# One chunk's x split moved ahead, LN centring one step later and mixers 24 steps apart, in a three-layer kernel on one core

## The chip, the cores and the metric

One core of one Trainium2 chip runs the whole program: landmark attention, an MLP block with a low-rank token mixer, and an MLP block with a Fourier mixer. The metric is the device time of one execution in microseconds (us). Engines are named TensorE (PE in the rows, PEld its weight loads), VectorE (DVE), ScalarE (ACT), GpSimd (POOL) and SyncE (SP), which issues nearly all DMAs. TensorE's granted clock stands in the rows as a share of 2.4 GHz.

## What is computed

Batch 8, sequence 576, width 512, MLP width 2048. The attention's output is x of the first block, and that block's output is x of the second:

```
x    = attn(q, k, v)                       # landmark attention, (8, 576, 512)
u1   = x + (x^T U V)^T                     # U 576x32, V 32x576
x1   = u1 + relu(u1 @ w11) @ w12
u2   = x1 + real(fft over sequence and width of x1)
un   = (u2 - mean(u2)) / sqrt(var(u2) + 1e-6)
out  = u2 + relu(un @ w21) @ w22
```

Everything is fp32. A product of two fp32 operands is made of three TensorE passes over operands that are split into a high and a low part (`hi = cast(src)`, `lo = src - hi`): low times high, high times low, high times high.

## The kernel before

**MLP passes.** The 4608 tokens are nine chunks of 512. Each block's MLP is run as two passes over half the hidden width, since the weights of one half fit in SBUF: passes 0 and 1 make x1, passes 2 and 3 make the output. `Mlp.stream(p)` is a generator that emits one pass in *MLP steps* (it yields after each): a chunk is sixteen of them, and every step is twelve TensorE matmuls of 512 columns. Steps 0 to 7 are the up projection (`up`, L213 to L215: weights times high x, low weights times high x, weights times low x; then relu on ScalarE, L217, and the low part of g on VectorE, L218). Steps 8 to 15 are the down projection, two steps for each of four output blocks d (L258 to L260), each block ended by an eviction from PSUM: L267 on VectorE in passes 1 and 3, L265 on ScalarE in pass 2. The matmul results go through three PSUM banks, so a bank must be empty again two steps after its last matmul.

**x of the next chunk.** `load` brings xf, four tiles of 128x512, in step 3 of passes 1 to 3. `split_x` makes high and low parts of one tile at each call: the cast L51 on ScalarE, the subtraction L52 on VectorE for tiles 0 and 2, on GpSimd for tiles 1 and 3. The generator `more` is called at each of the eight stops of the down projection; it is created at d == 2, so the four tiles are split in steps 12 to 15. The four x tiles are single: they come free when the up projection has read them.

**Mixers.** Beside passes 1 and 2 run eight `Mixer`s, one for each batch: load U (one batch of x1), fold over width and sequence (the Fourier transform's symmetry), small DFT matmuls, unfold, add, store u2, and the LN. `Mixer.steps()` gives each piece a number; `Slots` runs the pieces of number r in MLP step `first + r`, right after that step of the MLP. The numbers that matter here: 0 load U; 4 the folds over width (L692: even part on VectorE, odd part on GpSimd); 5 to 8 the fold over sequence (L702) and splits, among them of one row (L713, `rh`, `rl`); 8 to 13 the DFT over width; 14 to 18 that over the sequence; 17 to 19 unfold; 20 store. LN follows for two halves n of the sequence: `sum_u` at 20 + n (two additions on VectorE, L782 and L783), `centre` at 21 + n (a mean by a matmul with a constant, L787, and the subtraction L797 on VectorE), `sum_sq` at 22 + n (square L802 on ScalarE, sums on VectorE), `put` of the centred half at 23 + n, `deviation` at 24 + n (again a mean, then L810 to L813 on ScalarE and L814 on GpSimd), `newton` at 25 + n (L818, L819 on VectorE) and `put_scale` at 26 + n. U has one buffer, so the next batch's load waits for this batch's second `centre`.

**Staging.** A third generator, `later`, converts the weights of the next passes from float64 to split fp32 (`stage`, `convert`): per weight tile four VectorE instructions (L96, L97, L100, L103) with L101 on ScalarE and L104 on GpSimd, then L106 on VectorE, then a split. It is advanced twice in steps divisible by 4 and once in others, and a weight tile takes ten advances, that is eight MLP steps.

**What sets the order.** Each engine runs its own instructions in the order in which they are emitted: MLP step, mixer pieces, constants' set-up, staging. An instruction that has to wait holds up all behind it on its engine. The mixers are put down by

```
for b in range(B):
    slots.add(34 + 22 * b, Mixer(fp, psb, f, b).steps())
```

counted from the first step of pass 1; a pass has 144 steps, so mixer 5 begins with pass 2. In what follows "mixer b" is that of batch b, and "mixer step r" the MLP step in which its pieces of number r are emitted.

Of the kernel before, what the change touches and what calls it, by code (L numbers as in the profile page):

```python
# [39 lines left out]
def body(ctx: ExitStack, tc: tile.TileContext, qT, kT, vn, mU, mV, w11, w12, w21, w22,  # L40
# [88 lines left out]
    def rows(d):  # L129
        return slice(d * P, (d + 1) * P)  # L130
# [33 lines left out]
    class Mlp:  # L164
# [57 lines left out]
        def stream(self, p, tail=None):  # L222
            x_src, res_src, dst, _ = self.passes[p]
            for c in range(NCH):
# [3 lines left out]
                after = (p, c + 1) if not last else (p + 1, 0) if p + 1 < len(self.passes) else None  # L228
# [20 lines left out]
                for d in range(4):  # L249
                    if d == 1 and after and p == 0:  # L250
                        self.xf = self.load(after[1], self.passes[after[0]][0])
                    if d == 2 and after:
                        more = self.split_x(self.xf)
                    ps = self.bank()
                    for k in range(HM):
                        gh, gl = g[k][:, 0, :], g[k][:, 1, :]
                        wh, wl = w2[k][:, 0, rows(d)], w2[k][:, 1, rows(d)]
                        nc.tensor.matmul(ps, wh, gh, start=k == 0, stop=False)  # L258
                        nc.tensor.matmul(ps, wl, gh, start=False, stop=False)  # L259
                        nc.tensor.matmul(ps, wh, gl, start=False, stop=k == HM - 1)  # L260
                        if k == HM // 2 - 1:
                            next(more, 0)
                            yield 1
                    if res_src is None:
                        nc.scalar.copy(res[d], ps)  # L265
                    else:
                        nc.vector.tensor_tensor(res[d], ps, res[d], op=ALU.add)  # L267
                    if tail:
                        nc.vector.tensor_tensor(res[d], res[d], sc, op=ALU.mult)
                        nc.vector.tensor_tensor(res[d], res[d], skip[d], op=ALU.add)  # L270
                    dst.put(c, d, res[d])
                    next(more, 0)
                    yield 1
# [396 lines left out]
    class Mixer:  # L670
# [156 lines left out]
        def steps(self):  # L827
            yield from ((0, self.load), (4, lambda: self.fold_d("e")), (4, lambda: self.fold_d("o")),
                        (5, lambda: self.fold_t("e")), (6, lambda: self.fold_split("e")), (6, self.fold_row),
                        (7, lambda: self.fold_t("o")), (8, lambda: self.fold_split("o")))  # L830
            yield from ((8 + 3 * (nm == "o") + i, lambda nm=nm, i=i: self.over_d(nm, i)) for nm in "eo"
                        for i in range(3))
            yield from ((14, self.top_row), (15, lambda: self.odd(0)), (16, lambda: self.even(0)),
                        (17, lambda: self.unfold(0)), (17, lambda: self.unfold(2)), (17, lambda: self.odd(1)),
                        (18, lambda: self.even(1)), (19, lambda: self.unfold(1)), (19, lambda: self.unfold(3)),
                        (20, self.store))
            for n in range(2):
                yield from ((20 + n, lambda n=n: self.sum_u(n)), (21 + n, lambda n=n: self.centre(n)),
                            (22 + n, lambda n=n: self.sum_sq(n)), (24 + n, lambda n=n: self.deviation(n)),
                            (23 + n, lambda n=n: self.put(n)),  # L840
                            (25 + n, lambda n=n: self.newton(n)), (26 + n, lambda n=n: self.put_scale(n)))

        LAST = 28

    def pool(name, **k):
        return tc.tile_pool(name=name, bufs=1, reuse_waits="tile", **k)
# [35 lines left out]
    N = NCH * STEPS  # L882
    with pool("mm") as mp, pool("pm", space=PSUM) as pm:
# [33 lines left out]
        with pool("aa") as ap_, pool("ac") as ac, pool("cv0") as cv0, pool("pt", space=PSUM) as psb:  # L917
            t = {}
            batches = [Batch(ap_, psb, t, b) for b in range(B)]
            slots = Slots()  # L920
# [30 lines left out]
        with tc.manual_schedule(), pool("cv") as cv:  # L951
            with pool("fp") as fp, pool("fc") as fc, pool("pf", space=PSUM) as psb:
                f = {}
                slots = Slots()
                for b in range(B):
                    slots.add(34 + 22 * b, Mixer(fp, psb, f, b).steps())
                later, gen = staging(cv, 2), mlp.stream(1)
                setup = fourier_setup(f, fc, fp)
                for s in range(N + 80):
                    if s == N:  # L960
                        some(later, 999)
                        some(gen, 9)
                        later, gen = staging(cv, 3), mlp.stream(2)
                    next(gen)
                    slots.run(s)
                    next(setup, 0)
                    some(later, 2 if s % 4 == 0 else 1)
            assert not slots.at
            for s in range(N - 80):
                next(gen)  # L970
                some(later, 2 if s % 4 == 0 else 1)
            some(later, 999)
            some(gen, 9)
            with pool("tl") as mlp.tail_pool:
                for _ in mlp.stream(3, (Scales(rs), U2)):
                    pass
# [75 lines left out]
```

## Time and profile before

| | us |
|---|---|
| median of 3 runs | 2014.88 |
| the three runs | 2014.88, 2016.48, 2009.8 |
| the profiled execution | 2012.54 |
| its span, first to last instruction | 2010.8 |

In the span TensorE is busy for 1900.4 us (95%), its weight loads for 1540.5, VectorE for 948.5, ScalarE for 552.9 and GpSimd for 356.1; the mean granted clock is 0.976. Consecutive matmuls overlap, and a busy engine need not be at its peak rate, so how long a step takes is read from the starts of its matmuls. Below, a stretch always runs from the first matmul of one MLP step to that of another; pass 1 begins at 682.14 us of the span, pass 2 at 1164.50 and pass 3 at 1613.29. A timeline row gives the start, the duration, engine, line and operation, what is written and read, and in brackets how long the engine was idle before it and what ended that.

### The profile page before, as it was taken

How to read it: one execution, taken by the hardware profiler on the slowest of the kernel's cores; microseconds unless marked ns; L12 is line 12 of the kernel's file. 1: busy time of each engine (PE TensorE's matmuls, PEld its weight loads, DVE VectorE, ACT ScalarE, POOL GpSimd, SP SyncE). 2: the span in 40 equal slices, each digit the busy share in tenths (PEclk: the TensorE clock that was granted, in tenths of full speed). 3: DMA queues.
4: the chain of work that ended last, by engine and by line, in shares of the span. 5: the costliest groups of instructions: out<-in, count | busy, mean ns of one | idle time of the engine just before them, and what ended most of it. 6: DMA issues, size and time to landing. Idle time of an engine off the chain costs nothing.

```text
span 2010.8 us, 27221 instructions
## 1 busy us (share of the span) xinstructions
PE 1900.4 (95%) x10808; PEld 1540.5 (77%) x10808; DVE 948.5 (47%) x1628; ACT 552.9 (27%) x1145; POOL 356.1 (18%) x344
## 2 busy tenths in 40 slices
PE   3568999999999999999999999999999999999998
PEld 2356777777778888778878777888888888888887
DVE  6795465556433334555466355464422233333333
ACT  2333332333322222233233233333322211111110
POOL 2441011111111112122222121221211110001000
PEclk8689999999999999989999999999999999999999
DMA  6224335343333743344354463343232453432332
GB/s 245 88 102 128 120 108 171 112 145 107 103 125 127 235 134 134 102 158 143 123 169 144 155 228 106 115 158 130 91 105 90 141 178 114 131 96 90 94 100 74
DMA packets 145873, 262.33 MB, mean 130 GB/s; under 512 B 22768, under 2 KB 77904, under 8 KB 145744
## 3 DMA queue, kind: packets, MB, share of 16 engines
q1 hardware_dynamic: 141248, 251.14, 37.6%
q10 hardware_dynamic: 4496, 9.44, 1.2%
q8 instruction: 85, 1.39, 0.3%
q14 instruction: 44, 0.36, 0.1%
HBM read 166.93 MB, written 93.59 MB: 130 GB/s over the span
## 4 chain that ended last, share of the span: by engine, by line
PE 75%; DVE 8%; DMA 7%; issue 3%; ACT 2%; POOL 2%; ACTq 0%; SPq 0%; POOLq 0%; DVEq 0%
PE ps L215 12%; PE ps L213 12%; PE ps L214 12%; PE ps L258 10%; PE ps L260 10%; PE ps L259 10%; DMA u<-u1T 5%; PE ps_f L76 1%; PE ps_f L77 1%; PE ps_f L78 1%; PE ps_n L572 1%; PE ps_n L613 1%; POOL x L52 1%; DMA xf<-u 1%; PE ps_c L443 1%
## 5 line engine op out<-in xcount | busy, mean ns | idle before, releaser
L213 PE MATMUL ps<-x,w 128*128 128x512 f32 x1152 | 466.8, 405 | 3.9 <-ACT x L51 3.9
L215 PE MATMUL ps<-x,w 128*128 128x512 f32 x1152 | 455.7, 396 | 7.6 <-POOL x L52 7.0
L258 PE MATMUL ps<-g,w 128*128 128x512 f32 x1152 | 460.1, 399 | 0.9 <-DVE g L218 0.9
L214 PE MATMUL ps<-x,w 128*128 128x512 f32 x1152 | 453.5, 394 | 0.0
L260 PE MATMUL ps<-g,w 128*128 128x512 f32 x1152 | 449.7, 390 | 0.0
L259 PE MATMUL ps<-g,w 128*128 128x512 f32 x1152 | 448.8, 390 | 0.0
L218 DVE SCALAR_TENSOR_TENSOR g<-ps,g 128x512 fp32r<-128x512 f32 x288 | 199.0, 691 | 463.0 <-ACT g L217 462.1
L217 ACT ACTIVATE g<-ps 128x512 fp32r<-128x512 f32 x288 | 171.9, 597 | 681.1 <-PE ps L215 680.6
L215 PEld LDWEIGHTS ps<-x,w 128*128 128x128 f32 x1152 | 218.9, 190 | 61.1 <-POOL x L52 12.8
L213 PEld LDWEIGHTS ps<-x,w 128*128 128x128 f32 x1152 | 219.3, 190 | 53.1 <-ACT x L51 4.9
L258 PEld LDWEIGHTS ps<-g,w 128*128 128x128 f32 x1152 | 216.3, 188 | 49.4 <-issue 4.4
L214 PEld LDWEIGHTS ps<-x,w 128*128 128x128 f32 x1152 | 219.5, 191 | 43.6
L260 PEld LDWEIGHTS ps<-g,w 128*128 128x128 f32 x1152 | 216.2, 188 | 46.7
L259 PEld LDWEIGHTS ps<-g,w 128*128 128x128 f32 x1152 | 216.5, 188 | 42.9
L104 POOL TENSOR_TENSOR cvp<-cvp,cva 128x512 f32<-128x512 f32 x64 | 83.3, 1301 | 692.0 <-DVE cvp L103 692.0
L267 DVE TENSOR_TENSOR xf<-ps,xf 128x512 f32<-128x512 f32 x108 | 74.4, 689 | 259.7 <-PE ps L260 256.8
L52 POOL TENSOR_TENSOR x<-xf,x 128x512 fp32r<-128x512 f32 x70 | 94.3, 1351 | 375.0 <-ACT x L51 373.4
L52 DVE TENSOR_TENSOR x<-xf,x 128x512 fp32r<-128x512 f32 x74 | 57.5, 779 | 114.8 <-ACT x L51 114.4
L51 ACT CAST x<-xf 128x512 fp32r<-128x512 f32 x144 | 85.4, 618 | 59.0 <-DMA xf<-u 58.8
L52 POOL TENSOR_TENSOR stg<-cva,stg 128x512 fp32r<-128x512 f32 x48 | 66.6, 1387 | 125.7 <-ACT stg L51 124.4
L572 PE MATMUL ps_n<-ry 128*128 128x192 f32 (+1 forms) x192 | 43.3, 352 | 35.1 <-DVE ry L576 35.1
L101 ACT ACTIVATE wraw<-wraw 128x512 f32<-128x512 f32 x50 | 34.1, 681 | 140.8 <-DVE cva L97 140.7
(276 smaller groups left out, 1750.6 us busy)
## 6 DMA issues: line engine op xcount, KB each, us to landing
wraw<-w SPq DMA_DIRECT2D x50, 512.0 KB
d<-stg SPq DMA_DIRECT2D x48, 512.0 KB
w<-d SPq DMA_DIRECT2D x48, 512.0 KB
y<-xf SPq DMA_DIRECT2D x72, 256.0 KB
xf<-y SPq DMA_DIRECT2D x72, 256.0 KB
U<-x SPq DMA_DIRECT2D x8, 1152.0 KB
u<-U SPq DMA_DIRECT2D x8, 1152.0 KB
un<-Z SPq DMA_DIRECT2D x16, 576.0 KB
```

The costliest lines, as they stand in the source:

```text
L51: nc.scalar.copy(hi, src)
L52: (eng or nc.vector).tensor_tensor(lo, src, f32(hi), op=ALU.subtract)
L104: nc.gpsimd.tensor_tensor(pf, pf, af, op=ALU.add)
L213: nc.tensor.matmul(ps, wh, xh, start=k == 0, stop=False)
L214: nc.tensor.matmul(ps, wl, xh, start=False, stop=False)
L215: nc.tensor.matmul(ps, wh, xl, start=False, stop=k == 3)
L217: nc.scalar.activation(g[:, 0, :], ps, AF.Relu)
L218: nc.vector.scalar_tensor_tensor(out=g[:, 1, :], in0=ps, scalar=0.0, in1=f32(g[:, 0, :]), op0=ALU.max, op1=ALU.subtract)
L258: nc.tensor.matmul(ps, wh, gh, start=k == 0, stop=False)
L259: nc.tensor.matmul(ps, wl, gh, start=False, stop=False)
L260: nc.tensor.matmul(ps, wh, gl, start=False, stop=k == HM - 1)
L267: nc.vector.tensor_tensor(res[d], ps, res[d], op=ALU.add)
```

## The change

In passes 1 to 3 the generator that splits x of the next chunk is created at the first block of the down projection instead of the third, so its four tiles are split in steps 8 to 11 (pass 0 keeps 12 to 15). In the mixer `centre` and all that follows it come one step later, while `sum_u` stays. The mixers begin at step 33 and then every 24 steps, instead of at 34 and every 22; the loops' bounds follow.

```diff
--- before.py
+++ after.py
@@ -249,7 +249,7 @@
                 for d in range(4):
                     if d == 1 and after and p == 0:
                         self.xf = self.load(after[1], self.passes[after[0]][0])
-                    if d == 2 and after:
+                    if d == (0 if p else 2) and after:
                         more = self.split_x(self.xf)
                     ps = self.bank()
                     for k in range(HM):
@@ -835,10 +835,10 @@
                         (18, lambda: self.even(1)), (19, lambda: self.unfold(1)), (19, lambda: self.unfold(3)),
                         (20, self.store))
             for n in range(2):
-                yield from ((20 + n, lambda n=n: self.sum_u(n)), (21 + n, lambda n=n: self.centre(n)),
-                            (22 + n, lambda n=n: self.sum_sq(n)), (24 + n, lambda n=n: self.deviation(n)),
-                            (23 + n, lambda n=n: self.put(n)),
-                            (25 + n, lambda n=n: self.newton(n)), (26 + n, lambda n=n: self.put_scale(n)))
+                yield from ((20 + n, lambda n=n: self.sum_u(n)), (22 + n, lambda n=n: self.centre(n)),
+                            (23 + n, lambda n=n: self.sum_sq(n)), (25 + n, lambda n=n: self.deviation(n)),
+                            (24 + n, lambda n=n: self.put(n)), (26 + n, lambda n=n: self.newton(n)),
+                            (27 + n, lambda n=n: self.put_scale(n)))
 
         LAST = 28
 
@@ -953,10 +953,10 @@
                 f = {}
                 slots = Slots()
                 for b in range(B):
-                    slots.add(34 + 22 * b, Mixer(fp, psb, f, b).steps())
+                    slots.add(33 + 24 * b, Mixer(fp, psb, f, b).steps())
                 later, gen = staging(cv, 2), mlp.stream(1)
                 setup = fourier_setup(f, fc, fp)
-                for s in range(N + 80):
+                for s in range(N + 88):
                     if s == N:
                         some(later, 999)
                         some(gen, 9)
@@ -966,7 +966,7 @@
                     next(setup, 0)
                     some(later, 2 if s % 4 == 0 else 1)
             assert not slots.at
-            for s in range(N - 80):
+            for s in range(N - 88):
                 next(gen)
                 some(later, 2 if s % 4 == 0 else 1)
             some(later, 999)
```

**ScalarE, the end of pass 1's chunk 3** (L51 `x<-xf` is the cast of x, `stg` and L101 are staging, L802 and L810 to L813 the LN, `he` and `rh` the fold's splits, L217 the first relu of chunk 4). Before:

```order
L51 CAST x<-xf 128x512
L101 ACTIVATE wraw<-wraw 128x512
L51 CAST x<-xf 128x512
L699 COPY cc<-big 128x2x2
L51 CAST x<-xf 128x512
L51 CAST he<-cc 128x578
L714 COPY top<-U 1x2
L51 CAST rh<-top 1x289
L51 CAST stg<-cva 128x512
L51 CAST x<-xf 128x512
L699 COPY cc<-big 128x2x2
L217 ACTIVATE g<-ps 128x512
```

Now, from the last relu of chunk 3 on:

```order
L217 ACTIVATE g<-ps 128x512
L51 CAST x<-xf 128x512
L802 ACTIVATE big<-Z 128x1152
L51 CAST x<-xf 128x512
L802 ACTIVATE big<-Z 128x1152
L51 CAST x<-xf 128x512
L810 ACTIVATE r<-ps_l,eps 128x288
L811 ACTIVATE v<-ps_l,eps 128x288
L812 ACTIVATE r<-r 128x288
L813 ACTIVATE w<-r 128x288
L51 CAST x<-xf 128x512
```

The four casts moved from among staging and fold to among the LN of the mixer before, and the staging and the fold come behind them.

**VectorE, the LN of one mixer in the up projection** (`cc<-U` and `cc<-cc` are `sum_u`, L797 `centre`, L218 the MLP's). Before (mixer 5):

```order
L782 TENSOR_TENSOR cc<-U 128x2x288
L783 TENSOR_TENSOR cc<-cc 128x288
L96 TENSOR_SCALAR cva<-wraw 128x512
L97 SCALAR_TENSOR_TENSOR cva<-wraw,cva 128x512
L100 TENSOR_SCALAR cvp<-cva 128x512
L103 SCALAR_TENSOR_TENSOR cvp<-wraw,cvp 128x512
L218 SCALAR_TENSOR_TENSOR g<-ps,g 128x512
L797 TENSOR_TENSOR Z<-U,ps_l 128x1152
L782 TENSOR_TENSOR cc<-U 128x2x288
L783 TENSOR_TENSOR cc<-cc 128x288
```

Now (mixer 2):

```order
L782 TENSOR_TENSOR cc<-U 128x2x288
L783 TENSOR_TENSOR cc<-cc 128x288
L106 SCALAR_TENSOR_TENSOR cva<-wraw,cvp 128x512
L218 SCALAR_TENSOR_TENSOR g<-ps,g 128x512
L782 TENSOR_TENSOR cc<-U 128x2x288
L783 TENSOR_TENSOR cc<-cc 128x288
L218 SCALAR_TENSOR_TENSOR g<-ps,g 128x512
L797 TENSOR_TENSOR Z<-U,ps_l 128x1152
```

The second half's sums now stand ahead of the first half's subtraction; staging's four conversions come before both.

**VectorE, the beginning of a fold in the up projection** (L692 the fold, L96 to L106 the staging, L818 and L819 Newton of the mixer before). Before (mixer 5):

```order
L218 SCALAR_TENSOR_TENSOR g<-ps,g 128x512
L818 TENSOR_SCALAR w<-w 128x288
L819 TENSOR_TENSOR r<-r,w 128x288
L692 TENSOR_TENSOR big<-U 128x1152
L96 TENSOR_SCALAR cva<-wraw 128x512
L97 SCALAR_TENSOR_TENSOR cva<-wraw,cva 128x512
L100 TENSOR_SCALAR cvp<-cva 128x512
L103 SCALAR_TENSOR_TENSOR cvp<-wraw,cvp 128x512
L218 SCALAR_TENSOR_TENSOR g<-ps,g 128x512
```

Now (mixer 2):

```order
L818 TENSOR_SCALAR w<-w 128x288
L819 TENSOR_TENSOR r<-r,w 128x288
L96 TENSOR_SCALAR cva<-wraw 128x512
L97 SCALAR_TENSOR_TENSOR cva<-wraw,cva 128x512
L100 TENSOR_SCALAR cvp<-cva 128x512
L103 SCALAR_TENSOR_TENSOR cvp<-wraw,cvp 128x512
L218 SCALAR_TENSOR_TENSOR g<-ps,g 128x512
L692 TENSOR_TENSOR big<-U 128x1152
L106 SCALAR_TENSOR_TENSOR cva<-wraw,cvp 128x512
```

The conversions went from behind the fold to a step ahead of it, and Newton ends before them.

## Rows read from the trace of the kernel before

**Rows 1.** The page, part 4: the chain that ended last, by engine.

```profile
PE 75%; DVE 8%; DMA 7%; issue 3%; ACT 2%; POOL 2%; ACTq 0%; SPq 0%; POOLq 0%; DVEq 0%
```

**Rows 2.** Stretches: length, busy of each engine (x instructions), TensorE clock, DMA share, GB/s.

```profile
682.14:1164.50 482.36, 472.41 (x2199) 387.19 (x2197) 244.42 (x377) 135.95 (x269) 108.61 (x90) 0.98 0.44 147
1164.50:1613.29 448.79, 442.81 (x2021) 361.70 (x2020) 195.51 (x291) 139.00 (x265) 92.12 (x75) 1.00 0.37 128
1657.27:1700.79 43.52, 43.52 (x193) 36.04 (x192) 15.04 (x22) 6.85 (x12) 2.54 (x2) 1.00 0.33 103
1033.00:1099.54 66.54, 66.49 (x324) 54.73 (x323) 37.53 (x63) 21.64 (x43) 14.54 (x13) 1.00 0.42 143
872.79:889.83 17.04, 13.02 (x41) 8.82 (x39) 7.64 (x11) 4.59 (x10) 6.16 (x6) 0.70 0.66 216
1033.00:1041.04 8.04, 8.04 (x41) 6.32 (x40) 5.67 (x11) 3.29 (x7) 3.02 (x3) 1.00 0.16 54
1102.26:1113.43 11.17, 8.36 (x25) 6.39 (x24) 8.15 (x9) 1.88 (x5) 5.41 (x4) 0.71 0.43 121
1437.75:1443.56 5.81, 5.74 (x26) 4.43 (x25) 0.69 (x1) 1.70 (x3) 1.28 (x1) 1.00 0.71 238
1238.25:1251.40 13.15, 11.16 (x41) 8.47 (x40) 11.60 (x16) 4.14 (x6) 2.97 (x2) 0.87 0.24 90
1317.82:1327.20 9.38, 9.38 (x41) 7.44 (x40) 5.87 (x9) 2.28 (x3) 0.00 (x0) 1.00 0.37 140
1185.70:1198.48 12.78, 11.31 (x53) 8.47 (x51) 9.13 (x14) 5.48 (x13) 5.37 (x5) 1.00 0.49 151
```

**Rows 3.** Grouped lines: busy, mean ns of one | idle before, who ended it.

```profile
L215 PE MATMUL ps<-x,w 128*128 128x512 f32 x1152 | 455.7, 396 | 7.6 <-POOL x L52 7.0 <-DVE x L52 0.2
```

**Rows 4.** Timeline, TensorE: the second half's mean of mixer 5.

```profile
1246.49 0.95 PE L787 MATMUL ps_l<-cc,ones 128*128 128x288 f32 x2 [1.99 <-DVE cc L783]
```

**Rows 5.** Timeline, TensorE, start of pass 1 chunk 4: start, us, instruction [idle before].

```profile
878.75 0.80 PE L213 MATMUL ps<-x,w 128*128 128x512 f32 x1 [2.09 <-ACT x L51]
...
886.21 0.63 PE L213 MATMUL ps<-x,w 128*128 128x512 f32 x1
```

**Rows 6.** Timeline, ScalarE, the same place.

```profile
870.61 0.68 ACT L101 ACTIVATE wraw<-wraw 128x512 f32<-128x512 f32 x1 [6.34 <-DVE cva L97]
871.19 0.60 ACT L51 CAST x<-xf 128x512 fp32r<-128x512 f32 x1
...
878.08 0.61 ACT L51 CAST x<-xf 128x512 fp32r<-128x512 f32 x1
```

**Rows 7.** Timeline, GpSimd: the folds of mixers 1 and 5.

```profile
864.60 3.32 POOL L692 TENSOR_TENSOR big<-U 128x576 f32<-128x576 f32 x2
...
1182.90 4.10 POOL L692 TENSOR_TENSOR big<-U 128x576 f32<-128x576 f32 x2 [2.23 <-DMA U<-x]
```

**Rows 8.** Timeline, VectorE: Newton of mixer 0, both halves.

```profile
862.59 0.46 DVE L819 TENSOR_TENSOR r<-r,w 128x288 f32<-128x288 f32 x1
...
866.68 1.56 DVE L819 TENSOR_TENSOR r<-r,w 128x288 f32<-128x288 f32 x1
```

**Rows 9.** Timeline, ScalarE, pass 3 chunk 1, after step 7.

```profile
1679.73 2.17 ACT L51 CAST x<-xf 128x512 fp32r<-128x512 f32 x4
```

**Rows 10.** Timeline, SP's queue, pass 2 chunk 0.

```profile
1177.04 10.53 SPq L140 DMA_DIRECT2D xf<-un  x8
```

**Rows 11.** Timeline, VectorE: LN of mixer 5.

```profile
1243.83 1.35 DVE L797 TENSOR_TENSOR Z<-U,ps_l 128x1152 f32<-128x1152 f32 x1
...
1245.88 0.46 DVE L783 TENSOR_TENSOR cc<-cc 128x288 f32<-128x288 f32 x1
```

**Rows 12.** Timeline, ScalarE: staging beside the fold of mixer 5.

```profile
1187.59 0.68 ACT L101 ACTIVATE wraw<-wraw 128x512 f32<-128x512 f32 x1 [6.53 <-DVE cva L97]
1188.16 0.58 ACT L217 ACTIVATE g<-ps 128x512 fp32r<-128x512 f32 x1
```

**Rows 13.** Timeline, VectorE: the fold of mixer 0.

```profile
788.02 1.90 DVE L106 SCALAR_TENSOR_TENSOR cva<-wraw,cvp 128x512 f32<-128x512 f32 x1 [0.74 <-POOL cvp L104]
```

## The prediction

> **What bounds the kernel now.** First the chain of waits on the page: TensorE holds three quarters of it, VectorE 8% [rows 1]. So I ask where TensorE stands still. Second, stretches cut at MLP step boundaries [rows 2]. A chunk of pass 3 (sixteen steps, no side work) takes 43.52 us at full clock, so a bare step is 2.72 us. Mixer 3's steps 8 to 26 take 66.54 us with TensorE busy for 66.49: nineteen bare steps (51.68) and 14.86 of the mixer's own matmuls. Passes 1 and 2 take 482.36 + 448.79 = 931.15 us and hold 288 steps and eight mixers: 288 x 2.72 + 8 x 14.86 = 902.2. The difference, **29.0 us**, is all the standing still in these two passes. Pass 0, whose work the change leaves as it is, and pass 3, which runs bare steps, I leave out.
>
> Third, by whom: the grouped lines name the low half of x (L215 waits for L52) [rows 3], the timeline the LN sums (L787 waits for L783) [rows 4]. The stretches show four kinds [rows 2]:
> - Chunk 4 of pass 1, first two steps: 17.04 us where mixer 3's like pair takes 8.04: 9.0 lost. Chunk 8: 11.17 against 2 x 2.72: 5.7 lost. In both the granted clock falls to about 0.7.
> - The starts of pass 2's last five chunks: 5.81 us for two steps, 0.37 lost each.
> - One LN mean: three steps take 13.15 us, mixer 6's same three 9.38: 3.8 lost, again at a lower clock.
> - Mixer 5's steps 7 to 9: 12.78 against 2.72 + 8.04: 2.0 lost.
>
> Together 9.0 + 5.7 + 1.9 + 3.8 + 2.0 = 22.4; the other 6.6 are shorter waits of the first and third kind.
>
> **Why chunk 4 waits.** TensorE waits 2.09 us for ScalarE's cast of x; afterwards a matmul takes 0.63 us [rows 5] where the mean is 0.40 [rows 3]: the 1.2 GHz level. ScalarE works in order. The second cast stood behind the staging's L101, before which ScalarE had idled 6.34 us for VectorE; the fourth began at 878.08, over 5 us into the chunk that needs it (872.79) [rows 6]. VectorE was late since GpSimd's fold (3.32 us [rows 7]) ran beside it: the same L819 took 0.46 us before and 1.56 during it [rows 8]. The chip's rule for this follows in the rivals.
>
> **The change, part by part.**
> 1. *Split from the end of the up projection.* At the 18 chunk ends of passes 1 and 2, four casts on ScalarE, two subtractions on VectorE and two on GpSimd move up four MLP steps; none is added. Four steps are at least 10.9 us more lead. The latest cast above was 8 us behind its place (878.08 against the start of step 15, 872.79 - 2.72 = 870.1), so it would be done before the chunk starts. They may run there: the x buffers are free once step 7's matmuls are done, and pass 3, where no other ScalarE work stands between, already shows its four casts together at that point [rows 9]. What could be missing instead is xf. Its latest loads that I found, in pass 2's first chunk, were issued from 1177.04 to 1187.6 [rows 10]; step 8 there begins no sooner than 1185.70 + 2.72 [rows 2], and its cast needs the first of the four tiles alone. Where a landing were late, ScalarE would stand for a few us with four steps to spare: zero. The evictions L267 and L265 that now follow a cast wait for one cast at most and have two steps. Gain: 9.0 + 5.7 + 1.9 = **16.6**.
> 2. *Centring one step later.* The stalled mean had its sums ready at 1245.88 + 0.46, and TensorE waited 1.99 us for them [rows 11, 4]. Before those sums VectorE had done the first half's subtraction L797 (1.35 us), which itself needs a mean. Now the second half's sums stand ahead of that subtraction, and each mean comes at least 2.72 us after its old place; the longest wait was 1.99. So waits of this kind end: **3.8**. The square, the second mean, Newton and the four DMAs of a mixer follow a step later at unchanged distances, and nobody in these passes needs them soon. On SP the first half's put now goes ahead of the next U load. That load waits for the second half's subtraction, formerly of its own step, now of the step before: one step more for the transfer, some bytes more ahead of it. A late U has cost GpSimd 2.23 us [rows 7]; between -2.2 and +2.2 I take zero, since the step gained (2.72) is longer than that wait.
> 3. *Mixers 24 steps apart.* Staging repeats every 8 steps, so with 24 every mixer meets it at the same place: the four VectorE conversions in mixer step 3, L106 in step 4. With 22 the conversions fell into steps 2, 4, 6 and 0 in turn. Mixers 1 and 5 had them in step 4, on top of the fold; these two hold the worst chunk start and the whole fourth kind, where ScalarE's L101 had idled 6.53 us with a relu behind it [rows 12]. Mixer 0, conversions in step 2, had L106 slowed by GpSimd (1.90 us) [rows 13] and lost nothing at its fold. Step 3 lies between; Newton of the mixer before now ends a step ahead of the fold, so I take mixer 0's side. Gain **2.0**; bounds: all gone, or 2.0 in each of the four mixers that now fold in the up phase, a loss of 6.
>
> Matmuls, casts and DMAs stay the same in number. With the shorter waits (6.6, of kinds that parts 1 and 2 end): 16.6 + 3.8 + 2.0 + 6.6 = **29.0**. The profiled execution took 2012.54 us: 1983.5. The median of the runs shown is 2.34 higher: **1986**.
>
> **Rivals.** A measurement here tells about 0.3% (6 us) from no change.
> - *Phase lock.* All mixers share one phase now, so a wait that this phase has is paid up to eight times. For: the fold chain hung on the staging in mixer 5. Against: mixer 0. Price 2.0 x 8 = 16: 2002.
> - *The split doesn't get free.* The casts now alternate with LN's squares and logarithms on ScalarE, which wait for TensorE in their turn; then part 1 brings little, and 3.8 + 2.0 + half of 6.6 = 9 stays: 2006. Against: each of these waits ends within two steps, and four were gained.
> - *Slower.* GpSimd's two subtractions per chunk end now run beside LN or the fold's tail on VectorE, 36 in all. Each may hold one VectorE instruction by 1.56 - 0.46 = 1.10 us [rows 8]; if all of it reached TensorE, 39.6 us come back: 2026. It decides only where VectorE is already behind by its slack, two steps or 5.4 us. Against: they were there before, on fold instructions with less slack. The Trainium skill, page "SBUF — State Buffer", section "Who interferes with whom", says that a VectorE instruction with two SBUF inputs contends with a GpSimd instruction that reads SBUF, and that the second to issue waits for the first to finish. By that rule such a hold comes at every such pair; the trace agrees on the contention (0.46 to 1.56), and shows no place where one hold alone stopped TensorE.
> - *Within 0.3%*, if several of these add up.
>
> **How the numbers follow.** Forecast (all parts work, under 6 us of new waits): 0.72, 1979 to 1992. Phase lock 0.12 and the split not free 0.06, both still faster by over 6 us. Within 0.3%: 0.05. Slower: 0.05. Faster so has 0.90. The range reaches from 1979 (the lowest run shown, 2009.8, less about 30) to 2002, the phase lock's price; it leaves out half of that rival, the second one and the last two.
>
> **What would show it.** Right: pass 2's last chunks take 43.5 us, with no late start; no wait of L215 or L213 on L52 or L51 after pass 0, none of L787 on L783; passes 1 and 2 together near 902 us; granted clock 1 in them throughout; ScalarE's casts of x in steps 8 to 12. Wrong: waits that come back every 24 steps (phase lock); L51 waiting for xf's DMA; L787 still waiting; a clock that falls at a new place.

## The result and the profile after

The changed kernel takes **1991.02 us** (median of four runs, 1987.04 to 1992.94) beside 2015.64 us for the kernel before (four runs, 2009.8 to 2016.48): ratio 0.9888, 95% interval 0.9872 to 0.9905. That is 1.1% faster, inside the range of 1979 to 2002 and above the predicted 1986. The profiled execution took 1992.94 us with a span of 1990.8.

First the chain, the answer to [rows 1]: TensorE now holds 82% of it instead of 75%.

```profile
PE 82%; DVE 6%; DMA 6%; ACT 2%; issue 1%; ACTq 0%; POOL 0%; SPq 0%; DVEq 0%; POOLq 0%
```

Next the stretches, the answer to [rows 2], with the same columns (length, then busy time and instructions of TensorE, its weight loads, VectorE, ScalarE and GpSimd, then granted clock, DMA share and GB/s). The rows are, in order: pass 1; pass 2; the first two steps of pass 1's chunk 4 (mixer 1's steps 7 and 8); the first two of its chunk 8; mixer 5's steps 7 and 8; steps 22 to 24 of mixer 0, with LN means; the same of mixer 1; mixer 0's step 23 alone; the last chunk of pass 2.

```profile
687.85:1148.39 460.54, 458.36 (x2160) 377.95 (x2159) 237.73 (x365) 134.60 (x264) 112.52 (x88) 1.00 0.45 151
1148.39:1593.84 445.45, 443.34 (x2060) 366.70 (x2058) 195.69 (x302) 142.26 (x271) 98.17 (x78) 1.00 0.39 131
878.00:884.65 6.65, 6.65 (x33) 5.35 (x32) 5.05 (x7) 2.88 (x8) 4.27 (x4) 1.00 0.54 168
1095.48:1101.72 6.24, 6.24 (x28) 5.05 (x27) 3.91 (x6) 1.65 (x2) 0.00 (x0) 1.00 0.71 179
1200.41:1207.06 6.65, 6.65 (x34) 5.36 (x32) 4.70 (x6) 3.40 (x8) 4.49 (x4) 1.00 0.55 178
850.01:860.61 10.60, 9.51 (x42) 7.44 (x41) 9.86 (x13) 3.90 (x6) 3.93 (x3) 1.00 0.41 143
931.25:940.49 9.24, 9.24 (x41) 7.52 (x40) 5.04 (x8) 2.24 (x3) 1.58 (x1) 1.00 0.85 280
853.01:857.62 4.61, 3.52 (x16) 2.55 (x15) 4.58 (x6) 1.65 (x4) 1.68 (x1) 1.00 0.43 128
1550.33:1593.84 43.51, 43.51 (x194) 36.04 (x192) 7.55 (x10) 9.20 (x16) 2.58 (x2) 1.00 0.47 157
```

Wherever the length equals TensorE's busy time, TensorE does not stand still. That now holds at the chunk starts, at mixer 5's fold and in pass 2's last chunk. The granted clock is 1.00 in both passes; it had fallen to about 0.7 at the worst chunk starts. Passes 1 and 2 took 931.15 us and take 460.54 + 445.45 = 905.99, so 25.2 less. The span fell by 2010.8 - 1990.8 = 20.0 only: pass 0, where the change touches nothing, took 573.2 us in this execution and 566.8 before. Over the fourteen profiles of this study, all with the same work in pass 0, it takes 564.3 to 573.2. So variants are compared below by passes 1 and 2, beside their times.

In ScalarE's timeline the last cast of x for chunk 4 of pass 1 now begins 12.4 us before that chunk (878.00), where it began 5.3 us after its start [rows 2, 6]:

```profile
865.62 0.61 ACT L51 CAST x<-xf 128x512 fp32r<-128x512 f32 x1
```

One wait is new. Grouped lines of L215 and L787: L215's waits have shrunk from 7.6 us [rows 3] to 0.9, which lies in pass 0, and L787 no longer waits for L783 [rows 4] but for L797.

```profile
L215 PE MATMUL ps<-x,w 128*128 128x512 f32 x1152 | 452.7, 393 | 0.9 <-POOL x L52 0.9
L787 PE MATMUL ps_l<-cc,ones 128*128 128x288 f32 x64 | 21.1, 412 | 4.3 <-DVE Z L797 4.3
```

The timeline of VectorE, GpSimd and TensorE at mixer 0's step 23 shows how it comes about.

```profile
853.12 0.75 DVE L782 TENSOR_TENSOR cc<-U 128x576 f32<-128x576 f32 x1
853.90 1.43 DVE L783 TENSOR_TENSOR cc<-cc 128x288 f32<-128x288 f32 x1
855.25 0.68 DVE L218 SCALAR_TENSOR_TENSOR g<-ps,g 128x512 fp32r<-128x512 f32 x1
855.85 1.34 DVE L797 TENSOR_TENSOR Z<-U,ps_l 128x1152 f32<-128x1152 f32 x1
...
853.33 1.68 POOL L52 TENSOR_TENSOR stg<-cva,stg 128x512 fp32r<-128x512 f32 x1 [2.44 <-ACT stg L51]
...
857.25 0.75 PE L787 MATMUL ps_l<-cc,ones 128*128 128x288 f32 x2 [1.09 <-DVE Z L797]
```

The second half's mean writes `ps_l`, of which there is one buffer, and the first half's subtraction L797 has yet to read it. VectorE comes to L797 late: `sum_u` of the second half stands ahead of it, and there L783 takes 1.43 us where it took 0.46 [rows 11], beside GpSimd's split of a staged weight tile. The step takes 4.61 us; mixers 1, 3, 5 and 7 take 3.26 for it. So 1.35 us are lost in each of mixers 0, 2, 4 and 6 (1.29 in one of them): **5.3 us**. In these four the LN meets the up projection, where VectorE also makes g (L218); in the others it meets the down projection.

### The profile page after: what moved, and what is told of

It reads as the page before. It is cut to its first block, busy times and chain, and to the rows that moved or that the text cites. A ratio compares the mean times of both kernels' runs of the same rounds, so it can differ in the third digit from the quotient of the medians.

```text
span 1990.8 us, 27199 instructions
## 1 busy us (share of the span) xinstructions
PE 1893.4 (95%) x10808; PEld 1540.8 (77%) x10808; DVE 940.8 (47%) x1628; ACT 554.7 (28%) x1145; POOL 365.8 (18%) x344
## 3 DMA queue, kind: packets, MB, share of 16 engines
q8 instruction: 85, 1.39, 0.3%
## 4 chain that ended last, share of the span: by engine, by line
PE 82%; DVE 6%; DMA 6%; ACT 2%; issue 1%; ACTq 0%; POOL 0%; SPq 0%; DVEq 0%; POOLq 0%
PE ps L213 13%; PE ps L215 12%; PE ps L214 12%; PE ps L258 11%; PE ps L260 11%; PE ps L259 11%; DMA u<-u1T 5%; PE ps_f L77 1%; PE ps_f L76 1%; PE ps_f L78 1%; PE ps_n L613 1%; PE ps_n L572 1%; DMA xf<-u 1%; PE ps_c L443 1%; PE ps_l L787 1%
## 5 line engine op out<-in xcount | busy, mean ns | idle before, releaser
L215 PE MATMUL ps<-x,w 128*128 128x512 f32 x1152 | 452.7, 393 | 0.9 <-POOL x L52 0.9
L218 DVE SCALAR_TENSOR_TENSOR g<-ps,g 128x512 fp32r<-128x512 f32 x288 | 198.8, 690 | 472.6 <-ACT g L217 471.9
L217 ACT ACTIVATE g<-ps 128x512 fp32r<-128x512 f32 x288 | 171.9, 597 | 660.0 <-PE ps L215 659.6
L215 PEld LDWEIGHTS ps<-x,w 128*128 128x128 f32 x1152 | 218.0, 189 | 49.1 <-POOL x L52 1.4
L104 POOL TENSOR_TENSOR cvp<-cvp,cva 128x512 f32<-128x512 f32 x64 | 86.0, 1344 | 556.6 <-DVE cvp L103 556.6
L51 ACT CAST x<-xf 128x512 fp32r<-128x512 f32 x144 | 85.2, 618 | 59.8 <-DMA xf<-u 59.0
L101 ACT ACTIVATE wraw<-wraw 128x512 f32<-128x512 f32 x50 | 34.0, 680 | 136.9 <-DVE cva L97 134.4
```

Source lines behind the costliest of these rows:

```text
L51: nc.scalar.copy(hi, src)
L104: nc.gpsimd.tensor_tensor(pf, pf, af, op=ALU.add)
L215: nc.tensor.matmul(ps, wh, xl, start=False, stop=k == 3)
L217: nc.scalar.activation(g[:, 0, :], ps, AF.Relu)
L218: nc.vector.scalar_tensor_tensor(out=g[:, 1, :], in0=ps, scalar=0.0, in1=f32(g[:, 0, :]), op0=ALU.max, op1=ALU.subtract)
```

## The experiments

Passes 1 and 2 of each variant are the two stretches from its own trace, added. A loss in a step is that step's length less the shortest of the eight mixers at the same mixer step, or less 2.72 us where no mixer has work. Ratios are to the kernel before, run beside each. Each variant has one trace, so differences of its passes have no interval; pass 3, with the same work in all, takes 397.0 to 397.5 us in them.

### The parts one by one and in pairs

Part 1 alone:

```diff
-                    if d == 2 and after:
+                    if d == (0 if p else 2) and after:
```

> The kernel before with part 1 alone (x split from the end of the up projection on; centring and period as before). Theory (the casts were late, and four steps of lead cover it): the late chunk starts go, 16.6 us of the listed ones and some of the shorter ones, about 18.7 by the excess of all chunk-start steps over the cleanest of their kind; passes 1 and 2 together fall from 931.2 to about 912 us, TensorE's waits on L51 and L52 after pass 0 end, the waits of L787 for L783 stay. Time about 1996 us. Rival (the split doesn't get free, since its casts now stand between the LN's squares): passes 1 and 2 at 925 us or more, time 2008 or more, with L213 or L215 still waiting in pass 1.

Measured: 1992.43 us, ratio 0.991 (0.9891 to 0.9929).

```profile
680.93:1147.53 466.60, 464.51 (x2198) 382.59 (x2197) 242.53 (x377) 135.25 (x269) 108.08 (x90) 1.00 0.45 152
1147.53:1592.63 445.10, 440.80 (x2021) 362.29 (x2020) 192.29 (x291) 138.97 (x266) 92.77 (x76) 1.00 0.37 129
871.58:879.71 8.13, 8.08 (x42) 6.32 (x40) 5.06 (x9) 3.76 (x9) 2.90 (x4) 1.00 0.51 170
```

Passes 1 and 2 together: 911.7, so 19.5 less, as the theory had it; chunk 4's first two steps take 8.13 us instead of 17.04 [rows 2]. No chunk of passes 1 and 2 starts late any more, and the LN's means still wait. The rival falls.

Part 2 alone (the lines of `steps()` in the diff ahead of the prediction; the first of them stands for all):

```diff
-                yield from ((20 + n, lambda n=n: self.sum_u(n)), (21 + n, lambda n=n: self.centre(n)),
+                yield from ((20 + n, lambda n=n: self.sum_u(n)), (22 + n, lambda n=n: self.centre(n)),
```

> The kernel before with part 2 alone (centring and what follows it one step later; split and period as before). Theory: the waits of the LN means for their sums end, 8.4 us of passes 1 and 2 (3.8 of it the one listed), so 931.2 becomes about 923 us and the time about 2007; the late chunk starts stay. Rival: Newton then falls a step later, in steps 4 and 5 of the next mixer, which is where the next fold begins; VectorE is later there, the casts that wait behind its staging too, and the chunk starts lose what the means gain: passes 1 and 2 at 930 us or more.

Measured: 2013.15 us, ratio 1.0014 (1.0003 to 1.0024); passes 1 and 2 take 931.9. The rival holds in its number and in where the time goes: the means' waits fall from 8.4 us to 3.2, but the first step of chunk 8 loses 6.5 us instead of 3.3, chunk 4's starts 10.2 instead of 9.0, and mixer 5's fold 3.8 instead of 2.0. That Newton is what makes them late is not shown: at chunk 8 TensorE waits 5.58 us (2.81 before) for GpSimd's split of x, and mixer 5's fold on VectorE waits 1.76 us (0.30 before) for U.

Part 3 alone:

```diff
-                    slots.add(34 + 22 * b, Mixer(fp, psb, f, b).steps())
+                    slots.add(33 + 24 * b, Mixer(fp, psb, f, b).steps())
```

> The kernel before with part 3 alone (mixers 24 steps apart from step 33 on; split and centring as before). Theory (part 3 only takes the staging's conversions off the fold of mixers 1 and 5): the 2.0 us of mixer 5's fold go, and the worst chunk start, which hung on the same conversions; passes 1 and 2 between 918 and 929 us, time 2003 to 2013. Rival (phase lock: the split, still in chunk steps 12 to 15, now meets the fold of all four mixers that start at chunk step 9, steps 4 to 6 of theirs): a late chunk start after each of these four at up to 5.7 us, 23 us, passes 1 and 2 near 940 us or more, time 2024 or more.

Measured: 2012.8 us, ratio 1.0007 (0.9996 to 1.0018); passes 1 and 2 take 928.5, inside the theory's range, yet part of the rival is there too. Mixer 5's fold wait is gone and the late chunk starts shrink from 18.7 us to 9 (about 2 us at each of the four that meet a fold). But the LN means now lose some 14 us instead of 8.4, the same 2.1 us at the first mean of all four even mixers. VectorE's timeline at mixer 0's shows why:

```profile
845.80 0.69 DVE L103 SCALAR_TENSOR_TENSOR cvp<-wraw,cvp 128x512 f32<-128x512 uint32 x1
846.53 0.69 DVE L218 SCALAR_TENSOR_TENSOR g<-ps,g 128x512 fp32r<-128x512 f32 x1
847.13 1.39 DVE L782 TENSOR_TENSOR cc<-U 128x576 f32<-128x576 f32 x1
848.56 0.46 DVE L783 TENSOR_TENSOR cc<-cc 128x288 f32<-128x288 f32 x1
```

The staging's conversions (L96 to L103, the last of them shown) of mixer step 19 stand right ahead of `sum_u`. A common period locks that in. This is the phase lock of the prediction, and part 2 is what takes it away.

Parts 1 and 2 together, that is, the full change with the old period:

```diff
-                    slots.add(33 + 24 * b, Mixer(fp, psb, f, b).steps())
+                    slots.add(34 + 22 * b, Mixer(fp, psb, f, b).steps())
```

> Parts 1 and 2 together, without the period (mixers 22 apart from step 34 on). Theory (the parts add up, period worth 2.0): passes 1 and 2 at 931.2 - 18.7 - 8.4 = 904 us and mixer 5's fold still short of 2.0 us; time about 1988, as fast as the full change within 0.3%, and the 1.35 us wait at mixer step 23 that the full change has in four mixers is seen in none or one, as the mixers have no common phase. Rival (the period is what lets the other two work): passes 1 and 2 at 912 us or more, with chunk starts or means late again in mixers 1 and 5.

Measured: 1992.36 us, ratio 0.9905 (0.9885 to 0.9925); passes 1 and 2 take 465.2 + 443.7 = 908.9. This lies between the two theories. The wait at step 23 is seen once at 1.4 us and once at 0.3, as expected without a common phase; but mixer 5's fold loses 3.7 us, where it loses 1.8 with part 1 alone, and chunk 4's first step 1.6. In time, the full change can't be told from this pair (0.9888 and 0.9905, with intervals that overlap); in the two passes it is 2.9 us shorter.

The full change without part 1:

```diff
-                    if d == (0 if p else 2) and after:
+                    if d == 2 and after:
```

> The full change without part 1: x split where it was, in chunk steps 12 to 15; centring later and mixers 24 apart. Theory (part 1 is worth what late chunk starts remain when the period is changed): as in the run of part 3 alone, late starts after the four mixers that fold in chunk steps 13 to 17, about 2 us each, and 0.34 at the others, some 9 us, beside the 5.3 of the wait at mixer step 23; passes 1 and 2 at about 915 us, time near 2001. Rival (once the LN and the period are in place, the split has no more lateness to cover): passes 1 and 2 at 904 to 908 us.

Measured: 2013.83 us, ratio 1.0013 (1.0002 to 1.0025); passes 1 and 2 take 931.2, more than the theory's 915 and the rival's 904 to 908. The four chunk starts that meet a fold lose 5.5 to 6.5 us each, 23.9 together, where with part 3 alone they lost 2. A place that is bad with this phase is bad four times. Why part 2 makes these starts worse is not shown; at mixer 1's, TensorE waits 3.73 us for GpSimd's split of x, which stands behind GpSimd's fold, and that fold began 7.3 us after its step 4 (875.15 and 867.86), with part 3 alone 4.4 (872.62 and 868.18).

The full change without part 2 (`centre` at 21 + n again, and the rest with it):

```diff
-                yield from ((20 + n, lambda n=n: self.sum_u(n)), (22 + n, lambda n=n: self.centre(n)),
+                yield from ((20 + n, lambda n=n: self.sum_u(n)), (21 + n, lambda n=n: self.centre(n)),
```

> The full change without part 2: centring where it was. Theory (the LN's waits come from VectorE's sums being a step too close, and the common phase repeats them): as in the run of part 3 alone, first means wait 2.1 us in four mixers and second means 0.6 to 1.0, some 14 us, more than the 8.4 of the kernel before; passes 1 and 2 at about 914 us, time near 2000. Rival (these waits came from the split's casts and subtractions, which part 1 has moved away): passes 1 and 2 at 901 to 906 us.

Measured: 1996.78 us, ratio 0.9926 (0.9906 to 0.9945); passes 1 and 2 take 913.8, the theory's number: the first means lose 2.1 us in four mixers and the second ones 0.4 to 1.4, 12 us in all. So they do not come from the split.

| parts | passes 1 and 2, us |
|---|---|
| none | 931.2 |
| 1 | 911.7 |
| 2 | 931.9 |
| 3 | 928.5 |
| 1 and 2 | 908.9 |
| 1 and 3 | 913.8 |
| 2 and 3 | 931.2 |
| all | 906.0 |

The parts do not add. Part 1 carries 19.5 of 25.2. Part 2 is worth nothing alone, 2.8 beside part 1 and 7.8 beside parts 1 and 3. Part 3 costs 2.1 beside part 1 alone and gains 2.9 beside parts 1 and 2.

### How much lead the split needs

```diff
-                    if d == (0 if p else 2) and after:
+                    if d == (1 if p else 2) and after:
```

> The full change with the split of x two steps later (from the second tile of the down projection on instead of the first), so half of the lead. Theory (lead in time is what counts; in the kernel before the latest cast was 8 us behind its place): two steps are 5.4 us at least; with the period and the centring changed the casts are late by less than that, so passes 1 and 2 stay at 904 to 909 us, or lose up to 2.6 us per chunk start where ScalarE is as late as it was before chunk 4. Rival (the place counts: the casts must run before the LN's square or the fold of the mixer): late chunk starts in several chunks, passes 1 and 2 at 912 us or more.

Measured: 1989.1 us, ratio 0.9878 (0.9856 to 0.9901); passes 1 and 2 take 906.4. Half the lead does the same; no chunk starts late, and two mixers lose 0.2 us in their step 8. So, with the other two parts in place, it is the lead that counts, and two steps of it (at least 5.4 us) are enough.

### The new wait

Two PSUM buffers for the means:

```diff
-            ps = self.bank("l", 1)[:, 0:HS]
+            ps = self.bank("l", 2)[:, 0:HS]
```

> The full change with two PSUM buffers instead of one for the LN's means (L787's tile). Theory (the new wait at mixer step 23 of mixers 0, 2, 4, 6 is the second mean that waits until the first half's subtraction L797 has read the one buffer): L787 no longer waits for L797; these four steps fall from 4.6 to about 3.3 us, 5.3 us in all; passes 1 and 2 from 906.0 to about 901 us, time about 1986. Rival (the wait is VectorE's lateness and only moves to the next reader): passes 1 and 2 stay within 2 us of 906, with another line of the LN or L218's tile waited for in the same four mixers.

Measured: **1983.42 us**, ratio 0.9858 (0.9837 to 0.988). Its two passes:

```profile
682.31:1140.15 457.84, 457.84 (x2160) 378.06 (x2159) 239.68 (x365) 134.44 (x264) 112.35 (x88) 1.00 0.45 152
1140.15:1582.98 442.83, 442.83 (x2060) 366.81 (x2059) 195.44 (x302) 142.46 (x271) 98.12 (x78) 1.00 0.39 132
```

TensorE is busy for the whole of both: 900.7 us, 5.3 less than the full change, exactly the four steps. The theory holds. All its runs (1982.01 to 1986.16) lie below all of the full change's, which were not taken beside them; the two ratio intervals just overlap, and it is the trace that places the gain. Its median and its two passes are the shortest of the study.

Staging's split one step later, with the one buffer:

```diff
+        if late:
+            yield 1
...
-        yield from convert(cv, raw, st, bufs)
-        yield from wait(1)
+        yield from convert(cv, raw, st, bufs, bufs == 1)
+        yield from wait(int(bufs != 1))
```

> The full change with the staging's split of the next weights (GpSimd's and ScalarE's L52 on the stg tile) one step later in passes 1 and 2, so in mixer steps 6, 14 and 22 instead of 5, 13 and 21. Theory (the wait at mixer step 23 is there because VectorE's sums L783 took 1.43 us instead of 0.46 beside GpSimd's 1.68 us split): L783 is back at about 0.46 us, L797 starts about 1 us sooner, step 23 of mixers 0, 2, 4, 6 falls from 4.6 to about 3.6 us; passes 1 and 2 at about 902 us. Rival (GpSimd only moves its hold to the next VectorE instruction, the subtraction L797 or its neighbours in step 22): the step stays at 4.5 us or grows, passes 1 and 2 at 906 us or more.

Measured: 1986.94 us, ratio 0.9871 (0.985 to 0.9892); passes 1 and 2 take 902.1. VectorE, then GpSimd, at mixer 0's step 23 (the lines stand two higher in this kernel, so L785 is L783, and L799 is L797):

```profile
851.38 0.46 DVE L785 TENSOR_TENSOR cc<-cc 128x288 f32<-128x288 f32 x1
851.76 0.68 DVE L220 SCALAR_TENSOR_TENSOR g<-ps,g 128x512 fp32r<-128x512 f32 x1
852.36 1.34 DVE L799 TENSOR_TENSOR Z<-U,ps_l 128x1152 f32<-128x1152 f32 x1
...
851.60 1.40 POOL L52 TENSOR_TENSOR stg<-cva,stg 128x512 fp32r<-128x512 f32 x1 [3.23 <-ACT stg L51]
```

With GpSimd out of the way L785 takes 0.46 us, and the step's loss falls from 1.35 to 0.38: by 0.97, which is 1.43 - 0.46. GpSimd's 1.40 us now run beside L220 and L799, which stay at 0.68 and 1.34: the rival falls. So the hold beside GpSimd makes 0.97 of the 1.35, and the single buffer lets it through to TensorE.

### What part 3 does for the fold

Mixers 24 apart from step 40 on, so that the staging's conversions fall on step 4, where the folds start, in every mixer:

```diff
-                    slots.add(33 + 24 * b, Mixer(fp, psb, f, b).steps())
+                    slots.add(40 + 24 * b, Mixer(fp, psb, f, b).steps())
```

> The full change with the mixers started at step 40 instead of 33, still 24 apart: the staging's four conversions now fall into step 4 of every mixer, on top of the fold, as they did in mixers 1 and 5 of the kernel before. Theory (phase lock, and the place of the staging in the mixer decides): a fold wait like mixer 5's, 2.0 us, in the four mixers whose fold falls into the up projection, 8 us, or in all eight, 16 us; passes 1 and 2 at 914 to 922 us; the waits at mixer step 23 go, as the staging's split leaves step 21. Rival (what hurt before was the chunk's split beside the fold, and it is now elsewhere): no fold wait, passes 1 and 2 at 900 to 907 us.

Measured: 1987.99 us, ratio 0.9878 (0.9856 to 0.9901); passes 1 and 2 take 904.8. No fold waits: the rival holds in that, and the prediction's reason for part 3 falls. The wait at step 23 did not go, as I had expected it to: it is now 1.39 us in three odd mixers, where L104, another GpSimd instruction, runs beside the second half's L782 (1.40 us instead of 0.75).

What else stood at mixer 5's fold [rows 7]? GpSimd's L692 had waited 2.23 us for U's DMA. U has one buffer, so its load waits for the second subtraction of the mixer before; with part 2 and period 22 that comes a step later still (with parts 1 and 2 mixer 5's fold on VectorE waits 1.78 us for U, before it waited 0.30). The next run delays the load alone:

```diff
-            yield from ((0, self.load), (4, lambda: self.fold_d("e")), (4, lambda: self.fold_d("o")),
+            yield from ((3, self.load), (4, lambda: self.fold_d("e")), (4, lambda: self.fold_d("o")),
```

> The full change with each mixer's load of U issued in its step 3 instead of step 0. Theory (what part 3 gives the fold is time for this load: it waits for the subtraction of the mixer before, the single buffer's last reader, and took some 10 us from issue to fold): the folds begin 3 to 5 us later than in the full change, waiting for the DMA, and TensorE's wait at the fold's first matmul comes back at 2 to 4 us in most mixers; passes 1 and 2 at 920 to 938 us. Rival (part 3 helps by where the staging's conversions fall in a mixer, which this run leaves alone): passes 1 and 2 within 2 us of 906.

Measured: 1987.08 us, ratio 0.9884 (0.9856 to 0.9912); passes 1 and 2 take 906.3. Its VectorE timeline at mixer 1:

```profile
869.11 1.36 DVE L692 TENSOR_TENSOR big<-U 128x1152 f32<-128x1152 f32 x1 [1.66 <-DMA U<-x]
870.38 1.92 DVE L106 SCALAR_TENSOR_TENSOR cva<-wraw,cvp 128x512 f32<-128x512 f32 x1
872.23 1.98 DVE L702 TENSOR_TENSOR cc<-big 128x574 f32<-128x574 f32 x1
```

The folds do wait for the DMA now, and TensorE loses nothing but 0.36 us in one mixer: the theory falls. The last run has both edits, the start at 40 and the load in step 3:

```diff
-            yield from ((0, self.load), (4, lambda: self.fold_d("e")), (4, lambda: self.fold_d("o")),
+            yield from ((3, self.load), (4, lambda: self.fold_d("e")), (4, lambda: self.fold_d("o")),
...
-                    slots.add(33 + 24 * b, Mixer(fp, psb, f, b).steps())
+                    slots.add(40 + 24 * b, Mixer(fp, psb, f, b).steps())
```

> The full change with the mixers started at step 40 and each load of U issued in mixer step 3: both a late U and the staging's four conversions in mixer step 4, which each alone cost TensorE no more than 0.4 us. Theory (the fold wait of mixer 5 in the kernel before took both: a fold that starts late stands with the conversions in one row on VectorE, slowed by GpSimd, in the up projection where VectorE also has g to make): the fold waits come back in the odd mixers, which fold in the up projection, at 1.5 to 4 us each, 6 to 16 us; the even ones lose under 0.5; passes 1 and 2 at 911 to 921 us. Rival (neither is the cause; something else of the old phase, the x loads at the start of pass 2 say, was): at most 0.5 us in any mixer's steps 6 to 9, passes 1 and 2 at 903 to 908 us.

Measured: 2024.91 us, ratio 1.0063 (1.0046 to 1.008): slower than before. Passes 1 and 2 take 478.5 + 463.3 = 941.8, 37.0 more than with the start at 40 alone, while the late load alone cost 0.3. The two do not add. Steps 7 to 9 lose 2.0 to 8.1 us in seven of the eight mixers. VectorE, then TensorE, in mixer 1:

```profile
899.44 1.36 DVE L692 TENSOR_TENSOR big<-U 128x1152 f32<-128x1152 f32 x1 [5.22 <-DMA U<-x]
900.72 1.63 DVE L96 TENSOR_SCALAR cva<-wraw 128x512 uint32<-128x512 uint32 x1
902.38 1.77 DVE L97 SCALAR_TENSOR_TENSOR cva<-wraw,cva 128x512 uint32<-128x512 uint32 x1
904.18 0.43 DVE L100 TENSOR_SCALAR cvp<-cva 128x512 uint32<-128x512 uint32 x1
904.64 0.69 DVE L103 SCALAR_TENSOR_TENSOR cvp<-wraw,cvp 128x512 f32<-128x512 uint32 x1
905.36 0.69 DVE L218 SCALAR_TENSOR_TENSOR g<-ps,g 128x512 fp32r<-128x512 f32 x1
...
906.11 0.79 PE L258 MATMUL ps<-g,w 128*128 128x512 f32 x1 [5.09 <-DVE g L218]
```

L692 holds VectorE for 5.22 us until U is there; the conversions queue up behind it, L96 and L97 slowed (1.63 and 1.77 us, beside GpSimd's fold; 0.42 and 0.69 with the start at 40 alone), and g comes last, for which the down projection waits. In the kernel before, mixer 5's fold has the same wait at the same line:

```profile
1189.52 0.50 PE L258 MATMUL ps<-g,w 128*128 128x512 f32 x1 [0.94 <-DVE g L218]
```

Three cases side by side tell what mixer 5's wait took. In the kernel before its fold began 5.5 us after its step 4 (1182.79 and 1177.28) with the conversions right behind: 2.0 us lost. With the late load alone mixer 1's fold began 5.6 us late (869.11 and 863.53) with the conversions ahead of it: nothing. With the start at 40 alone the conversions stood behind a fold that had not waited: nothing. The last run itself has two more cases, the VectorE folds of mixers 4 and 5:

```profile
1159.82 1.36 DVE L692 TENSOR_TENSOR big<-U 128x1152 f32<-128x1152 f32 x1 [5.81 <-DMA U<-x]
1161.09 0.68 DVE L267 TENSOR_TENSOR xf<-ps,xf 128x512 f32<-128x512 f32 x1
...
1237.10 1.36 DVE L692 TENSOR_TENSOR big<-U 128x1152 f32<-128x1152 f32 x1 [0.84 <-DMA U<-x]
1238.37 1.66 DVE L96 TENSOR_SCALAR cva<-wraw 128x512 uint32<-128x512 uint32 x1
```

Mixer 4's fold waited 5.81 us for U and began 7.8 us after its step 4, as late as those of mixers 0, 2 and 6 (7.4 to 8.2 us), which lost 5.9 to 7.3 us at the same place of their chunks. But staging for pass 2 has ended by then, none of its work stands behind the fold, and mixer 4 lost nothing. Mixer 5's began only 5.1 us late, with conversions behind it, and lost 2.0, as in the kernel before. It took both, and part 3 removes both. My number for the last run (6 to 16 us, in the odd mixers alone) was too small. The even ones lose too: in mixer 0 TensorE stands 2.53 us for the cast `he` of the late fold. And the load went out later there than I had meant, behind twelve loads of xf on SP's queue (881.56 to 892.45), so mixer 1's fold began 9.5 us after step 4 (899.44 and 889.98). How much of the 37.0 that made stays open; mixer 4 shows that at its place a load so late costs nothing by itself.

## Why the prediction was right, and where it was off

- **Part 1** was put at 16.6 us, and with its share of the shorter waits, in the expectation of its own run, at about 18.7; alone it gave 19.5. The mechanism, casts behind late VectorE work, was the right one, and in the full change four steps were more than enough (two do).
- **Part 2** (3.8 and part of 6.6) is right as to the means that waited for their sums: none does in the full change. Its side effect on U's load, taken as zero, is zero only with period 24; with 22 mixer 5's fold waited longer for U and lost 3.8 us instead of 2.0. And the step "now the second half's sums stand ahead of that subtraction" was told as a pure gain. It puts the subtraction behind them, and the next mean needs the buffer that this subtraction reads. With the hold beside GpSimd this is the 5.3 us that came back, and the step of the prediction that failed.
- **Part 3**: 2.0 us at mixer 5's fold is what went, for a reason that was half right. Conversions in step 4 alone do no harm; together with a late U they do. That this term came out was in part luck.
- **Phase lock**, given 0.12 at 2.0 us in eight mixers, did come, in a smaller form and at another place: 1.35 us in four. With part 3 but without part 2 it costs 12 to 14 us at the means, near the price of 16; without part 1, 23.9 us at the chunk starts, above it. Two signs that the prediction had named for being wrong did show: waits that come back with the mixers (in every second one), and L787 still waiting, now for L797.
- **The sum**: 29.0 was forecast for passes 1 and 2 and 25.2 came. The new wait is 5.3; the floor is 900.7 instead of 902.2, which gives back 1.5. The forecast had allowed for under 6 us of new waits. Adding the parts happened to work for the whole, since it was counted against a floor; for single parts it fails, as the table shows.
- **Slower through GpSimd and VectorE**: the hold exists, at 0.97 us where 1.10 was the price, but the four that reached TensorE are staging's splits, none of the 36 subtractions of x that the rival counted. Two of those subtractions held an L783 as well (859.22 and 1020.45), and TensorE lost nothing there. In the full change's trace L783 takes 0.46 us in the 20 cases without GpSimd. Of the 12 beside it, it takes 1.43 or 1.44 in the 8 in which GpSimd's instruction had begun first, and 0.46 in the 4 in which L783 had begun first, by 0.02 or 0.03 us; L218 takes 0.68 or 0.69 in all 227 without and 61 with. The Trainium skill, page "SBUF — State Buffer", section "Who interferes with whom", says that a VectorE instruction with two SBUF inputs contends with a GpSimd instruction that reads SBUF, and one with at most one SBUF input, outside certain fast modes, does not. The trace agrees on both: L783 has both inputs in SBUF, L218 takes one from PSUM. It also agrees that the later one waits: GpSimd's split ran from 853.33 to 855.01, and L783, begun at 853.90, ended at 855.33; in all 8 cases L783 ended 0.31 or 0.32 us after GpSimd's instruction.
- The median lies 5.0 us above the forecast; 3.8 of that is what passes 1 and 2 fell short.

## What to carry to other kernels

Before a piece is moved behind another on an in-order engine, look up which single buffer it releases, and who waits for that buffer: a second PSUM buffer was worth 5.3 us here, and no other wait came with it. Side work with a common period meets the main loop at the same place each time, so one bad place is paid in every round and one good place costs nothing; choose the phase by trying the places, and see that the pieces which still collide have a buffer between them. A wait on an in-order queue costs by what stands behind it: a late load and a queue of conversions behind it each cost 0.4 us at most in a mixer, and the run with both, where the load also went out later, cost 37 us.

## What the runs showed that I had not expected

Without part 1, parts 2 and 3 gain nothing measurable (ratio 1.0013), though each takes away a wait that the trace shows. And pass 0 varies by 9 us between profiles (564.3 to 573.2) with the same work in it, more than any part but the first brings. It goes with the granted clock: over pass 0 this is 0.98 in the seven longest (569.1 to 573.2) and 0.99 in the seven others (564.3 to 566.8), while the time that TensorE stands still there, 22.9 to 26.4 us, does not follow the length. Why the clock was lower in some executions stays open.
